# Sparse attention into an ELU MLP on one core: PSUM pairs in neighbouring banks, GpSimd's clamps moved, its fills spread, loads reordered, and a new instruction queue

## The chip, the core and the metric

The kernel runs on one core of a Trainium2 chip. The core has five engines that each take instructions from a queue of their own in order: TensorE (PE, matrix products, with weight loads shown apart as PEld), VectorE (DVE), ScalarE (ACT), GpSimd (POOL) and SyncE (SP). Sixteen DMA engines move data between HBM and the on-chip memory SBUF. Matrix products are written to PSUM, eight banks of 512 float32 columns on 128 partitions. The metric is the time of one execution on the device in microseconds (us), median over runs.

## The reference: what is computed

Attention over 8 batches, 8 heads, 576 positions and 64 channels. Four heads see the last 32 positions, four see the earlier positions at distances that are multiples of 32. Its output is 4608 tokens of 512 channels, and goes through an MLP with an ELU.

```python
scores = (1 / sqrt(64)) * q @ k.T                  # q, k, v: (8, 8, 576, 64) float32
rel = pos[:, None] - pos[None, :]
mask_local   = (rel >= 0) & (rel < 32)             # heads 0 to 3
mask_strided = (rel >= 0) & (pos[None, :] % 32 == pos[:, None] % 32)   # heads 4 to 7
attn = softmax(where(mask, scores, -1e9))
x = (attn @ v) as (4608, 512)
h = x @ w_in                                       # w_in (512, 2048)
g = where(h > 0, h, exp(min(h, 0)) - 1)
out = g @ w_out                                    # w_out (2048, 512), out (4608, 512) float32
```

## The kernel before

Every position is put at a residue, so that the strided heads become dense blocks of 72 by 72 and the local heads become blocks of 96 queries against 128 keys. Attention gives xT, the transposed MLP input, in bf16. The MLP goes over 9 chunks of 512 tokens.

The order of all work is written out by hand in one string, ORDER. Each token of it issues the instructions of one step, and each engine gets its instructions in the order of the tokens. Waits are not written: the framework adds them where one engine's instruction touches what another's has touched. The first letter of a token is the step, and a last number is a PSUM bank or a pair of banks:

- S (scores, L418), e (exp, L425, ACT), m (mask, L432 and L438, DVE), O (values and row sums, L445 to L488), n and r (logarithm and reciprocal of the sums, L516 and L522, ACT), x (product into xT, L547, DVE). Each batch has two strided and two local pairs of heads, each in two halves: S.3l0.1.07 is batch 3, local, pair 0, half 1, in banks 0 and 7.
- a and b, or L (first MLP product, L595; L is both halves, four matmuls), h (exp, L603, ACT), i, j or p (the clamp exp(h)-1 to at most 0, on DVE, ACT or GpSimd: L612 or L610), g (maximum with h, L623, DVE). L.2.5.4 is chunk 2, feature block 5, bank 4.
- Z (second MLP product, L629, four of its sixteen steps: Z.1.3.2.6 is chunk 1, token block 3, part 2, bank 6), o (copy to SBUF, L635, ACT), t (store, L647, SP).
- Ls and Ll load q, k and v of the strided or local heads of a batch, issued on GpSimd. Ts and Tl transpose q and k by DMA, Ks and Kl copy the transposed keys into two zero-padded buffers (kps, kpl). W copies v between its row of ones. T and c, C transpose on TensorE for batches 0 and 1, which have no DMA transposes. w issues products of zeros.

PSUM is one tile of eight banks. A score token, and from batch 2 on a value token, writes two banks, and one exp, logarithm or product reads both as one operand:

```python
    def banks(s):
        i, j = int(s[0]), int(s[1])
        return ps[:, i:j + 1:j - i, 0:W]
```

All raw buffers of a kind are single, so batch b+1 loads after batch b has been transposed. Batch 1 has buffers of its own inside xT and g. Ahead of the queue GpSimd issues the first loads, makes the masks, issues the loads of LOADS (w_in in four parts, w_out in four, batch 1), and then fills the zero and one regions of the padded buffers.

Of the kernel before, what the change touches and what calls it, by code (L numbers as in the profile page):

```python
# [15 lines left out]
S = 576  # L16
D = 64
HG = 4
NS = 8
RS = S // NS  # L20
RP = 80
# [10 lines left out]
LOADS = ['wi0', 'wi1', 'wi2', 'wi3', 'wo0', 'wo1', 'qs1', 'ks1', 'vs1', 'ql1', 'kl1', 'vl1', 'wo2', 'wo3']  # L32
# [8 lines left out]
w.7.28 K.q.1 K.q.0 K.k.1 K.k.0 T.0s0.q.0 c.0s0.q T.0s0.k.1 T.0s1.q.2 c.0s0.k T.0s1.k.3 C.0s1.q  # L41
w.7.1 c.0s1.k S.0s0.0.45 S.0s0.1.67 e.0s0.0 S.0s1.0.01 e.0s0.1 S.0s1.1.23 m.0s0.0 T.0l0.q.4
e.0s1.0 m.0s0.1 O.0s0.0.56 e.0s1.1 c.0l0.q m.0s1.0 n.0s0.0 T.0l0.k.7 m.0s1.1 r.0s0.0 O.0s1.0.01
x.0s0.0 T.0l1.q.4 c.0l0.k n.0s1.0 r.0s1.0 O.0s1.1.23 V.0 S.0l0.0.56 n.0s1.1 x.0s1.0 T.0l1.k.7
c.0l1.q e.0l0.0 O.0s0.1.01 r.0s1.1 c.0l1.k S.0l0.1.45 n.0s0.1 x.0s1.1 w.6.1 r.0s0.1 m.0l0.0
S.0l1.1.67 e.0l0.1 x.0s0.1 S.0l1.0.23 e.0l1.1 m.0l0.1 O.0l0.0.01 e.0l1.0 m.0l1.1 O.0l0.1.45
n.0l0.0 m.0l1.0 O.0l1.1.67 r.0l0.0 n.0l0.1 O.0l1.0.23 x.0l0.0 r.0l0.1 a.0.0.0 n.0l1.0 x.0l0.1
a.0.1.1 r.0l1.0 a.0.2.4 n.0l1.1 x.0l1.0 a.0.3.5 r.0l1.1 a.0.4.2 x.0l1.1 a.0.5.3 b.0.0 b.0.1
h.0.0 b.0.2 h.0.1 b.0.3 i.0.0 g.0.0 b.0.4 h.0.3 b.0.5 i.0.1 h.0.4 a.0.6.6 i.0.3 g.0.1 b.0.6
h.0.5 a.0.7.7 g.0.3 h.0.2 b.0.7 j.0.5 a.0.8.0 i.0.2 i.0.4 a.0.9.1 h.0.6 g.0.4 b.0.8 h.0.7 g.0.5  # L50
a.0.10.5 j.0.7 a.0.11.2 g.0.2 a.0.12.3 h.0.8 g.0.7 b.0.9 j.0.6 b.0.10 i.0.8 h.0.9 g.0.6 b.0.11
h.0.10 b.0.12 g.0.8 a.0.13.4 h.0.12 i.0.10 a.0.14.7 g.0.10 h.0.11 Ll.2 b.0.13 b.0.14 i.0.12
j.0.9 g.0.12 a.0.15.6 h.0.13 T.1s1.k.0 g.0.9 b.0.15 h.0.14 i.0.11 T.1s0.k.5 T.1s0.q.3 g.0.11
h.0.15 Z.0.0.0.1 i.0.13 C.1s0.k i.0.14 T.1s1.q.2 g.0.14 C.1s0.q Z.0.0.1.1 i.0.15 C.1s1.q g.0.13
S.1s0.1.35 T.1l0.q.7 g.0.15 e.1s0.1 c.1s1.k S.1s0.0.24 c.1l0.q T.1l0.k.6 e.1s0.0 m.1s0.1
S.1s1.0.35 V.1 O.1s0.1.07 c.1l0.k e.1s1.0 Ls.2 T.1l1.q.2 n.1s0.1 m.1s1.0 S.1l0.1.46 r.1s0.1
m.1s0.0 C.1l1.q O.1s1.0.35 x.1s0.1 Z.0.0.2.1 n.1s1.0 r.1s1.0 O.1s0.0.07 e.1l0.1 x.1s1.0
T.1l1.k.2 n.1s0.0 m.1l0.1 S.1s1.1.35 r.1s0.0 c.1l1.k Z.0.0.3.1 e.1s1.1 x.1s0.0 Z.0.1.0.4 m.1s1.1
o.0.0 O.1s1.1.26 t.0.0 S.1l1.0.35 n.1s1.1 O.1l0.1.07 r.1s1.1 Z.0.1.1.4 n.1l0.1 x.1s1.1 e.1l1.0
Z.0.1.2.4 r.1l0.1 m.1l1.0 S.1l0.0.12 W.2 Ts.2 S.1l1.1.36 e.1l0.0 x.1l0.1 Z.0.1.3.4 e.1l1.1  # L60
m.1l0.0 O.1l1.0.05 o.0.1 m.1l1.1 O.1l0.0.17 n.1l1.0 O.1l1.1.23 r.1l1.0 Z.0.2.0.6 n.1l0.0 t.0.1
x.1l1.0 r.1l0.0 n.1l1.1 Z.0.2.1.6 x.1l0.0 r.1l1.1 Z.0.2.2.6 x.1l1.1 L.1.0.4 Ks.2 Ls.3 L.1.1.0
h.1.0 L.1.2.5 i.1.0 h.1.1 g.1.0 L.1.3.1 i.1.1 h.1.2 g.1.1 Z.0.2.3.6 p.1.2 h.1.3 i.1.3 S.2s0.0.27
o.0.2 g.1.3 S.2s0.1.34 L.1.4.0 e.2s0.0 t.0.2 g.1.2 e.2s0.1 L.1.5.6 m.2s0.0 h.1.4 m.2s0.1
O.2s0.0.12 j.1.4 L.1.6.7 Tl.2 n.2s0.0 g.1.4 O.2s0.1.35 r.2s0.0 Z.0.3.0.4 n.2s0.1 x.2s0.0
Z.0.3.1.4 r.2s0.1 S.2s1.0.01 h.1.5 L.1.7.2 x.2s0.1 e.2s1.0 i.1.5 L.1.8.3 g.1.5 h.1.7 h.1.6 i.1.7
L.1.9.5 g.1.7 h.1.8 p.1.6 L.1.10.0 m.2s1.0 h.1.9 g.1.6 O.2s1.0.16 h.1.10 Z.0.3.2.4 i.1.8 g.1.8
n.2s1.0 S.2s1.1.27 i.1.10 r.2s1.0 Z.0.3.3.4 Kl.2 Ll.3 g.1.10 e.2s1.1 L.1.11.3 x.2s1.0 o.0.3 Ts.3
m.2s1.1 L.1.12.0 h.1.11 i.1.9 g.1.9 O.2s1.1.27 h.1.12 L.1.13.1 i.1.11 g.1.11 n.2s1.1 S.2l0.0.46
i.1.12 r.2s1.1 L.1.14.5 g.1.12 t.0.3 h.1.13 x.2s1.1 L.1.15.3 e.2l0.0 i.1.13 S.2l1.0.02 m.2l0.0  # L70
h.1.15 S.2l0.1.47 Z.1.0.0.6 g.1.13 e.2l0.1 i.1.15 h.1.14 g.1.15 O.2l0.0.14 Z.1.0.1.6 j.1.14
m.2l0.1 Ks.3 n.2l0.0 g.1.14 O.2l0.1.37 r.2l0.0 Z.1.0.2.6 W.3 n.2l0.1 x.2l0.0 Ls.4 Z.1.0.3.6
r.2l0.1 S.2l1.1.15 e.2l1.0 Z.1.1.0.4 x.2l0.1 e.2l1.1 m.2l1.0 S.3s0.1.02 S.3s0.0.37 o.1.0 m.2l1.1
O.2l1.0.15 e.3s0.0 Z.1.1.1.4 t.1.0 n.2l1.0 m.3s0.0 O.2l1.1.36 Z.1.1.2.4 n.2l1.1 Z.1.1.3.4
r.2l1.1 r.2l1.0 x.2l1.1 Z.1.2.0.7 e.3s0.1 x.2l1.0 O.3s0.0.36 o.1.1 S.3s1.0.02 m.3s0.1 n.3s0.0
L.2.0.1 t.1.1 r.3s0.0 L.2.1.5 h.2.0 x.3s0.0 L.2.2.4 e.3s1.0 i.2.0 g.2.0 h.2.1 L.2.3.3 Tl.3 h.2.2
i.2.1 g.2.1 O.3s0.1.06 h.2.3 S.3s1.1.12 i.2.2 n.3s0.1 L.2.4.5 i.2.3 g.2.2 r.3s0.1 Z.1.2.1.7
g.2.3 h.2.4 x.3s0.1 L.2.5.4 e.3s1.1 Ts.4 i.2.4 L.2.6.3 g.2.4 h.2.5 m.3s1.1 L.2.7.0 i.2.5 h.2.6
g.2.5 O.3s1.1.16 p.2.6 h.2.7 L.2.8.2 m.3s1.0 n.3s1.1 g.2.6 O.3s1.0.45 Z.1.2.2.7 r.3s1.1 W.4
n.3s1.0 x.3s1.1 L.2.9.3 Kl.3 Ll.4 r.3s1.0 Z.1.2.3.7 j.2.7 x.3s1.0 h.2.8 L.2.10.1 g.2.7 Ks.4  # L80
h.2.9 Z.1.3.0.6 o.1.2 i.2.9 g.2.9 h.2.10 t.1.2 S.3l0.0.45 S.3l0.1.07 i.2.10 e.3l0.0 L.2.11.3
g.2.10 e.3l0.1 m.3l0.0 S.3l1.0.45 Z.1.3.1.6 m.3l0.1 e.3l1.0 h.2.11 O.3l0.0.01 m.3l1.0 O.3l0.1.47
L.2.12.5 n.3l0.0 i.2.11 g.2.11 r.3l0.0 Z.1.3.2.6 p.2.8 n.3l0.1 x.3l0.0 L.2.13.3 r.3l0.1 Ls.5
g.2.8 h.2.12 O.3l1.0.01 x.3l0.1 Z.1.3.3.6 n.3l1.0 i.2.12 S.3l1.1.24 r.3l1.0 g.2.12 L.2.14.7
e.3l1.1 x.3l1.0 L.2.15.5 h.2.13 m.3l1.1 o.1.3 Z.2.0.0.2 i.2.13 g.2.13 h.2.14 t.1.3 O.3l1.1.04
h.2.15 Z.2.0.1.2 i.2.14 g.2.14 n.3l1.1 Z.2.0.2.2 i.2.15 r.3l1.1 g.2.15 S.4s0.0.16 x.3l1.1
S.4s0.1.37 e.4s0.0 Z.2.0.3.2 e.4s0.1 m.4s0.0 L.3.0.5 o.2.0 m.4s0.1 L.3.1.0 t.2.0 h.3.0 L.3.2.4
i.3.0 h.3.1 g.3.0 L.3.3.1 i.3.1 h.3.2 g.3.1 Tl.4 O.4s0.0.36 h.3.3 i.3.2 Z.2.1.0.7 g.3.2 n.4s0.0
L.3.4.2 i.3.3 r.4s0.0 g.3.3 Z.2.1.1.7 x.4s0.0 h.3.4 O.4s0.1.05 i.3.4 L.3.5.4 g.3.4 n.4s0.1
Z.2.1.2.7 r.4s0.1 h.3.5 x.4s0.1 S.4s1.0.13 L.3.6.6 e.4s1.0 i.3.5 g.3.5 Z.2.1.3.7 h.3.6 m.4s1.0  # L90
L.3.7.2 i.3.6 o.2.1 g.3.6 O.4s1.0.05 Kl.4 Ll.5 h.3.7 S.4s1.1.13 Z.2.2.0.4 n.4s1.0 i.3.7 g.3.7
t.2.1 L.3.8.7 r.4s1.0 e.4s1.1 x.4s1.0 Ts.5 Z.2.2.1.4 h.3.8 m.4s1.1 L.3.9.6 i.3.8 g.3.8
O.4s1.1.12 h.3.9 S.4l0.0.03 W.5 Z.2.2.2.4 n.4s1.1 L.3.10.5 r.4s1.1 j.3.9 x.4s1.1 Z.2.2.3.4
e.4l0.0 g.3.9 S.4l0.1.17 h.3.10 L.3.11.2 m.4l0.0 o.2.2 i.3.10 O.4l0.0.03 g.3.10 e.4l0.1
Z.2.3.0.6 t.2.2 Ls.6 n.4l0.0 m.4l0.1 Ks.5 L.3.12.4 r.4l0.0 O.4l0.1.15 h.3.11 x.4l0.0 Z.2.3.1.6
n.4l0.1 i.3.11 S.4l1.0.07 g.3.11 r.4l0.1 L.3.13.3 h.3.12 x.4l0.1 Z.2.3.2.6 e.4l1.0 p.3.12 h.3.13
L.3.14.2 m.4l1.0 g.3.12 p.3.13 O.4l1.0.15 h.3.14 S.4l1.1.07 Z.2.3.3.6 g.3.13 n.4l1.0 i.3.14
L.3.15.4 r.4l1.0 g.3.14 e.4l1.1 Z.3.0.0.3 x.4l1.0 o.2.3 m.4l1.1 S.5s0.0.02 h.3.15 Z.3.0.1.3
t.2.3 e.5s0.0 i.3.15 O.4l1.1.17 g.3.15 Z.3.0.2.3 n.4l1.1 m.5s0.0 S.5s0.1.56 r.4l1.1 O.5s0.0.02
Tl.5 Z.3.0.3.3 x.4l1.1 n.5s0.0 Z.3.1.0.4 r.5s0.0 e.5s0.1 x.5s0.0 L.4.0.1 o.3.0 m.5s0.1 L.4.1.7  # L100
h.4.0 t.3.0 L.4.2.5 i.4.0 h.4.1 g.4.0 O.5s0.1.06 i.4.1 h.4.2 L.4.3.2 g.4.1 n.5s0.1 i.4.2
S.5s1.0.13 L.4.4.7 r.5s0.1 g.4.2 h.4.3 x.5s0.1 Z.3.1.1.4 e.5s1.0 i.4.3 L.4.5.5 g.4.3 h.4.4 Kl.5
Ll.6 m.5s1.0 Z.3.1.2.4 h.4.5 i.4.4 g.4.4 O.5s1.0.06 S.5s1.1.13 i.4.5 n.5s1.0 L.4.6.2 Ts.6 g.4.5
r.5s1.0 Z.3.1.3.4 e.5s1.1 x.5s1.0 L.4.7.7 h.4.6 m.5s1.1 o.3.1 i.4.6 O.5s1.1.15 g.4.6 h.4.7
Z.3.2.0.3 t.3.1 n.5s1.1 i.4.7 S.5l0.0.06 g.4.7 r.5s1.1 L.4.8.4 W.6 e.5l0.0 Z.3.2.1.3 x.5s1.1
h.4.8 m.5l0.0 L.4.9.2 i.4.8 g.4.8 Ks.6 Ls.7 O.5l0.0.07 h.4.9 Z.3.2.2.3 n.5l0.0 i.4.9 S.5l0.1.16
g.4.9 L.4.10.5 r.5l0.0 e.5l0.1 x.5l0.0 Z.3.2.3.3 h.4.10 m.5l0.1 L.4.11.4 o.3.2 i.4.10 g.4.10
O.5l0.1.12 t.3.2 h.4.11 S.5l1.0.06 Z.3.3.0.7 n.5l0.1 i.4.11 g.4.11 L.4.12.3 r.5l0.1 e.5l1.0
x.5l0.1 Z.3.3.1.7 h.4.12 m.5l1.0 L.4.13.5 i.4.12 g.4.12 O.5l1.0.04 h.4.13 S.5l1.1.16 Z.3.3.2.7
n.5l1.0 i.4.13 g.4.13 L.4.14.2 r.5l1.0 e.5l1.1 x.5l1.0 Z.3.3.3.7 h.4.14 m.5l1.1 L.4.15.3 o.3.3  # L110
i.4.14 Tl.6 g.4.14 O.5l1.1.15 h.4.15 Z.4.0.0.6 n.5l1.1 i.4.15 S.6s0.0.04 g.4.15 Z.4.0.1.6
r.5l1.1 e.6s0.0 x.5l1.1 S.6s0.1.27 Z.4.0.2.6 e.6s0.1 m.6s0.0 t.3.3 L.5.0.3 m.6s0.1 L.5.1.0 h.5.0
L.5.2.4 i.5.0 h.5.1 g.5.0 O.6s0.0.15 i.5.1 h.5.2 L.5.3.2 g.5.1 n.6s0.0 i.5.2 L.5.4.7 r.6s0.0
# [44 lines left out]
def kernel(  # L158
# [162 lines left out]
    for nm in LOADS:  # L321
        load(nm)
# [374 lines left out]
```

The softmax here doesn't subtract the row's maximum and nothing guards it: scores larger than these inputs give would overflow.

## Time and profile before

| quantity | value |
|---|---|
| time, median of 3 runs | 404.48 us (404.1 to 406.24) |
| span of the profiled run | 403.4 us |
| TensorE busy | 319.4 us, 79% |
| DVE busy | 237.0 us, 59% |
| ACT busy | 228.0 us, 57% |
| GpSimd busy | 106.2 us, 26% |
| mean granted TensorE clock | 0.961 |
| first MLP block, first batch 2 score, last xT product | 20.6, 74.1, ends 330.5 us |

Busy time is the time in which an engine has an instruction in work. In the lines of the profile a name is the program's tile, an arrow points from inputs to output, and "<-" in brackets names what ended the idle time before an instruction. In the view of waits the three numbers are the idle time in total, how often, and the longest.

### The profile page before, as it was taken

How to read it: one execution, taken by the hardware profiler on the slowest of the kernel's cores; microseconds unless marked ns; L12 is line 12 of the kernel's file. 1: busy time of each engine (PE TensorE's matmuls, PEld its weight loads, DVE VectorE, ACT ScalarE, POOL GpSimd, SP SyncE). 2: the span in 40 equal slices, each digit the busy share in tenths (PEclk: the TensorE clock that was granted, in tenths of full speed). 3: DMA queues.
4: the chain of work that ended last, by engine and by line, in shares of the span. 5: the costliest groups of instructions: out<-in, count | busy, mean ns of one | idle time of the engine just before them, and what ended most of it. 6: DMA issues, size and time to landing. Idle time of an engine off the chain costs nothing.

```text
span 403.4 us, 6126 instructions
## 1 busy us (share of the span) xinstructions
PE 319.4 (79%) x2263; PEld 161.2 (40%) x2302; DVE 237.0 (59%) x431; ACT 228.0 (57%) x388; POOL 106.2 (26%) x135
## 2 busy tenths in 40 slices
PE   6896788675778777778577686878988789999995
PEld 5643434332334343344233343434444334444442
DVE  3779835366416866665447665777467649639300
ACT  3785464464546775657556565676667756346121
POOL 8639932155000670432361205200000000000000
PEclk9999598899958999999999999999999999999999
DMA  8999996959714894898199819931421110110132
GB/s 151 189 206 189 132 159 130 156 63 175 117 26 120 125 132 80 137 150 143 49 117 134 165 41 144 83 89 51 99 72 28 26 28 0 48 58 0 53 80 79
DMA packets 110214, 40.59 MB, mean 101 GB/s; under 512 B 91784, under 2 KB 103752, under 8 KB 110184
## 3 DMA queue, kind: packets, MB, share of 16 engines
q0 software_dynamic: 71376, 18.75, 46.6%
q1 hardware_dynamic: 38808, 21.44, 22.8%
q8 instruction: 18, 0.29, 0.3%
q14 instruction: 12, 0.10, 0.1%
HBM read 38.03 MB, written 9.44 MB: 118 GB/s over the span
## 4 chain that ended last, share of the span: by engine, by line
PE 52%; DVE 18%; ACT 15%; DMA 8%; issue 4%; POOL 2%; SPq 0%; ACTq 0%; DVEq 0%; POOLq 0%
PE ps L629 24%; PE ps L595 21%; DVE xT L547 7%; ACT ln L516 6%; DVE g L623 5%; DVE he L612 5%; ACT e L425 4%; PE ps L418 4%; ACT he L603 2%; DMA kl<-in_k_dram 2%; ACT rc L522 2%; DMA kps<-kTs 2%; DMA qTs<-qs 2%; DMA ks<-in_k_dram 1%; PE ps L488 1%
## 5 line engine op out<-in xcount | busy, mean ns | idle before, releaser
L629 PE MATMUL ps<-w_out_sb,g 128*128 128x512 bf16 x557 | 143.6, 390 | 20.5 <-DVE xT L547 8.6
L595 PE MATMUL ps<-xT,w_in_sb 128*128 128x512 bf16 x556 | 137.5, 383 | 16.5 <-DVE xT L547 6.3
L603 ACT ACTIVATE he<-ps 128x512 f32<-128x512 f32 x144 | 84.4, 597 | 46.7 <-PE ps L595 36.0
L623 DVE TENSOR_TENSOR g<-he,ps 128x512 bf16<-128x512 bf16 x136 | 93.2, 687 | 21.7 <-ACT ln L516 7.3
L629 PEld LDWEIGHTS <-g 128*128 128x128 bf16 x576 | 54.4, 100 | 81.9 <-issue 30.7
L595 PEld LDWEIGHTS <-w_in_sb 128*128 128x128 bf16 x576 | 54.8, 98 | 79.7 <-issue 22.8
L612 DVE TENSOR_SCALAR he<-he 128x512 bf16<-128x512 f32 x130 | 64.0, 494 | 29.8 <-ACT he L603 29.4
L547 DVE TENSOR_TENSOR xT<-ps,rc 64x576 bf16<-64x576 f32 (+1 forms) x64 | 43.4, 680 | 62.9 <-ACT e L425 15.8
L425 ACT ACTIVATE e<-ps 72x576 bf16<-72x576 f32 (+1 forms) x64 | 40.9, 647 | 33.5 <-PE ps L418 13.7
L516 ACT ACTIVATE ln<-ps 64x576 f32<-64x576 f32 (+1 forms) x64 | 37.4, 584 | 38.0 <-PE ps L629 10.7
L635 ACT COPY osb<-ps 128x512 f32<-128x512 f32 x36 | 21.1, 585 | 40.1 <-PE ps L629 36.5
L522 ACT ACTIVATE rc<-ln 64x576 f32<-64x576 f32 (+1 forms) x64 | 39.7, 621 | 2.0
L245 POOL DMA_DIRECT2D ql<-in_q_dram x24 | 20.1, 845 | 46.5 <-DMA qTl<-ql 46.5
L612 POOL TENSOR_SCALAR he<-he 128x512 bf16<-128x512 f32 x6 | 12.0, 2004 | 48.8 <-ACT he L603 48.8
L418 PE MATMUL ps<-qTs,kps 128*128 128x72 bf16 x192 | 10.6, 198 | 15.7 <-DVE xT L547 5.7
L252 POOL DMA_DIRECT2D kl<-in_k_dram x24 | 18.1, 786 | 0.0
L432 DVE TENSOR_TENSOR pm<-e,mask_s 72x576 bf16<-72x576 bf16 x32 | 14.5, 461 | 5.9 <-ACT e L425 5.3
L438 DVE TENSOR_TENSOR pm<-e,mask_l 128x576 bf16<-128x576 bf16 x32 | 14.4, 454 | 5.9 <-ACT e L425 5.2
L418 PEld LDWEIGHTS <-kps 128*128 128x128 bf16 x192 | 9.1, 99 | 21.6 <-issue 18.8
L481 PE MATMUL ps<-pm,vsp 72*128 72x72 bf16 x192 | 11.0, 201 | 5.2 <-DVE xT L547 1.6
L481 PEld LDWEIGHTS <-vsp 72*128 72x128 bf16 x192 | 9.9, 101 | 12.6 <-issue 7.4
L418 PE MATMUL ps<-qTl,kpl 128*128 128x96 bf16 x144 | 10.3, 211 | 5.4 <-ACT ln L516 4.1
(87 smaller groups left out, 174.1 us busy)
## 6 DMA issues: line engine op xcount, KB each, us to landing
out_dram<-osb SPq DMA_DIRECT2D x32, 144.0 KB
vl<-in_v_dram POOLq DMA_DIRECT2D x8, 288.0 KB, 6.5
w_in_sb<-in_moe_w_in_dram POOLq DMA_DIRECT2D x4, 512.0 KB, 10.3
w_out_sb<-in_moe_w_out_dram POOLq DMA_DIRECT2D x4, 512.0 KB, 14.8
vs<-in_v_dram POOLq DMA_DIRECT2D x7, 288.0 KB, 7.7
kps<-kTs SPq DMA_DIRECT2D x12, 160.0 KB
ql<-in_q_dram POOLq DMA_DIRECT2D x24, 72.0 KB, 3.5
kl<-in_k_dram POOLq DMA_DIRECT2D x24, 72.0 KB, 3.7
```

What stands on the lines that cost most here:

```text
L418: nc.tensor.matmul(dst, lhsT=kt[pr, k0:k0 + 128], rhs=rhs, start=True, stop=True, skip_group_check=True)
L425: nc.scalar.activation(e[0:R], tiles.pop(("S", key, u))[0:R], ACT.Exp, scale=scale)
L481: nc.tensor.matmul(ov[:, x, j * RS:(j + 1) * RS], lhsT=vs_p[:, c0:c0 + 128], rhs=pm[0:RS, z, n0:n0 + RS], start=True, stop=True, skip_grou ...
L516: nc.scalar.activation(t, s_ps, ACT.Ln)
L522: nc.scalar.activation(t, tiles.pop(("ln", key, u)), ACT.Exp, scale=-1.0)
L547: nc.vector.tensor_mul(dst, o_ps, rc)
L595: nc.tensor.matmul(tiles["h", ch, m], lhsT=w_in_sb[:, c, m * 128:(m + 1) * 128], rhs=xT[:, c, ch * CHUNK:(ch + 1) * CHUNK], start=(c == 2) ...
L603: nc.scalar.activation(e, tiles["h", i[0], i[1]], ACT.Exp)
L612: eng.tensor_scalar(e1, e, scalar1=1.0, scalar2=1.0, op0=ALU.min, op1=ALU.subtract)
L623: nc.vector.tensor_tensor(dst, e1, h, op=ALU.max)
L629: nc.tensor.matmul(ops, lhsT=g[ch % 2][:, m, kk * 128:(kk + 1) * 128], rhs=w_out_sb[:, m, :], start=(m == 0), stop=(m == MC - 1), skip_gro ...
L635: nc.scalar.copy(o_sb, tiles.pop(("o", int(ch), int(kk))))
```

## The change

Five edits that go together:

1. Each pair of banks in ORDER is now two neighbours (i and i+1).
2. The six p tokens, clamps on GpSimd, are i tokens, clamps on DVE.
3. GpSimd's fills are taken apart and issued one after each load from batch 1's first on, rather than all behind the last load. The small loads that fill rows 72 to 79 of q and k (needed by the DMA transposes) move from batch 2's load to behind w_in.
4. All loads of batch 1 are issued ahead of w_out's.
5. The whole queue is ordered anew for this. Products of zeros go from 30 to 62, masks have five buffers for three, clamps three for four.

```diff
-LOADS = ['wi0', 'wi1', 'wi2', 'wi3', 'wo0', 'wo1', 'qs1', 'ks1', 'vs1', 'ql1', 'kl1', 'vl1', 'wo2', 'wo3']
+LOADS = ['wi0', 'wi1', 'wi2', 'wi3', 'qs1', 'ks1', 'vs1', 'ql1', 'kl1', 'vl1', 'wo0', 'wo1', 'wo2', 'wo3']
...
-L.1.3.1 i.1.1 h.1.2 g.1.1 Z.0.2.3.6 p.1.2 h.1.3 i.1.3 S.2s0.0.27
-o.0.2 g.1.3 S.2s0.1.34 L.1.4.0 e.2s0.0 t.0.2 g.1.2 e.2s0.1 L.1.5.6 m.2s0.0 h.1.4 m.2s0.1
+i.1.2 g.1.2 L.1.5.1 h.1.4 i.1.3 g.1.3 j.1.4 Z.0.2.3.7 h.1.5 g.1.4 S.2s0.0.45 o.0.2 S.2s0.1.23
+i.1.5 L.1.6.6 g.1.5 e.2s0.0 t.0.2 e.2s0.1 Z.0.3.0.7 m.2s0.0 h.1.6 m.2s0.1 O.2s0.0.01 L.1.7.2
...
-    p_pm = ctx.enter_context(tc.tile_pool(name="p_pm", bufs=3))
+    p_pm = ctx.enter_context(tc.tile_pool(name="p_pm", bufs=5))
...
-    p_he1 = ctx.enter_context(tc.tile_pool(name="p_he1", bufs=4))
+    p_he1 = ctx.enter_context(tc.tile_pool(name="p_he1", bufs=3))
...
-    for nm in LOADS:
-        load(nm)
-
-    for (c, z), t in kp.items():
...
+    fills = [lambda cz=cz: fill_kp(*cz) for cz in kp]
+    fills += [lambda a=a: fill_ones(*a)
+              for a in ((vl_t[0], HG * LB), (vl_t[1], HG * LB), (vs_p, HG * NS))]
+    for i, nm in enumerate(LOADS):
+        load(nm)
+        if nm == "wi3":
+            for a in (("qs", q), ("ks", k), ("ql", q)):
+                fill_rows(*a)
+        elif i >= 4 and fills:
+            fills.pop(0)()
...
     def load_str(b):
         for nm in ("qs", "ks", "vs"):
             load_runs(nm, int(b))
-        if int(b) == NPE:
-
-            for nm, x in (("qs", q), ("ks", k), ("ql", q)):
-                nc.gpsimd.dma_start(
-                    out=raw[nm][RS:RP].rearrange("p (h f) -> p h f", h=HG),
-                    in_=x[0, 0:HG].rearrange("h (p s) d -> p h (s d)", s=NS)[0:RP - RS])
```

## The prediction

> **What bounds the kernel now.** I read the page's engine shares first, then a table of stages, then what each engine waits for, then the timeline around single gaps.
>
> ```profile
> PE 319.4 (79%) x2263; PEld 161.2 (40%) x2302; DVE 237.0 (59%) x431; ACT 228.0 (57%) x388; POOL 106.2 (26%) x135
> ```
>
> No engine is full. TensorE is nearest, so the question is where it stands still. The stage table (window, its length, busy us and instructions of PE, PEld, DVE, ACT, POOL, granted clock, DMA share, GB/s):
>
> ```profile
> 0.00:20.00 20.00, 14.66 (x248) 12.28 (x250) 11.04 (x30) 11.69 (x22) 15.47 (x29) 1.00 1.16 170
> 20.00:74.00 54.00, 41.43 (x354) 21.18 (x357) 36.27 (x60) 30.44 (x62) 30.57 (x39) 0.87 1.24 167
> 74.00:331.00 257.00, 195.75 (x1357) 97.15 (x1383) 156.78 (x277) 159.74 (x261) 60.11 (x67) 0.97 0.70 96
> 331.00:399.00 68.00, 67.56 (x308) 30.63 (x313) 32.96 (x64) 25.56 (x43) 0.00 (x0) 1.00 0.17 47
> ```
>
> From 331 on only the two MLP products are left and TensorE is full: that stage can't shrink. From 74 to 331, where the attention of batches 2 to 7 runs between MLP blocks, it is idle for over 60 us, with DVE and ACT at 61% and 62% and DMA far below its 1.24. That is the signature of waits, not of work. The view of waits says for whom:
>
> ```profile
> PE ps L629 <- DVE xT L547: 8.6, 7, 2.1
> PE ps L418 <- ACT ln L516: 9.5, 9, 2.0
> PE ps L629 <- ACT e L425: 6.4, 9, 0.9
> PE ps L595 <- DVE xT L547: 6.3, 8, 1.2
> ACT he L603 <- DVE xT L547: 7.4, 7, 2.0
> ```
>
> These are odd pairs. The second MLP product (L629) reads g and w_out; nothing that writes xT or e feeds it. It can wait for them only over a PSUM bank. One such gap on the timeline:
>
> ```profile
> 147.95 0.65 ACT L516 ACTIVATE ln<-ps 64x576 f32<-64x576 f32 x1 [0.57 <-PE ps L629]
> 148.62 0.42 PE L488 MATMUL ps<-pm,vl 128*128 128x96 bf16 x6
> 149.96 0.75 DVE L547 TENSOR_TENSOR xT<-ps,rc 64x576 bf16<-64x576 f32 x1 [1.20 <-ACT he L603]
> 150.76 1.02 PE L629 MATMUL ps<-w_out_sb,g 128*128 128x512 bf16 x4 [1.72 <-DVE xT L547]
> ```
>
> In the queue the xT instruction is x.3l0.1, which reads the pair 47 (banks 4 and 7), and the L629 block is Z.1.3.3.6, which writes bank 6. They share no bank; bank 6 lies between 4 and 7. TensorE stood for 1.72 us until that read ended. I laid the queue's tokens beside the trace's instructions for the whole kernel: in 181 cases the last reader of a pair that merely spans a token's bank ends over 0.1 us after everything that the token truly needs, and in 174 of them the token starts within 0.15 us of that end. So a pair read as ps[:, i:j+1:j-i] counts as all banks from i to j. Of TensorE's 43.3 us between tokens from 125 to 335, 41.7 us end at such a reader; from 60 to 125 it is 10.0 of 14.1. Together 52 us. The slack it destroys is on all engines, so ACT and DVE queues run late too.
>
> Two things cost time before 74. First the fills:
>
> ```profile
> 36.91 5.02 DVE L612 TENSOR_SCALAR he<-he 128x512 bf16<-128x512 f32 x1
> 36.95 1.38 POOL L331 MEMSET vl<- 128x1536 bf16 x1
> 38.35 1.38 POOL L331 MEMSET vl<- 128x1536 bf16 x1
> 39.76 1.80 POOL L331 MEMSET vsp<- 72x2048 bf16 x1
> 42.71 0.64 PE L382 MATMUL ps<-identity,xT 72*128 72x72 bf16 x8 [4.63 <-DVE g L623]
> ```
>
> A clamp that takes 0.42 us elsewhere takes 5.02, exactly while GpSimd fills back to back, and TensorE waits 4.63 us behind it. Second, batch 2's padded keys:
>
> ```profile
> 66.94 7.48 DMA kps<-kTs
> 74.07 0.19 PE L418 MATMUL ps<-qTs,kps 128*128 128x72 bf16 x1 [2.77 <-DMA kps<-kTs]
> ```
>
> **The Trainium skill.** "PSUM — Partial Sum Buffer", section PSUM bank collisions, says to guard by bank; the hardware neither arbitrates nor stalls. The stalls here thus come from waits in the program, and the trace agrees: they end with the reader. "SBUF — State Buffer", Who interferes with whom, says that DVE in a two-port mode (tensor_scalar can enter one) and GpSimd exclude each other for whole instructions; the 5.02 against 0.42 us agrees. "TensorE: Matmul & The Clock Gate", Part 1, says that an idle window of about 3.4 us halves the clock; the 0.87 of stage 20 to 74 agrees.
>
> **The change part by part.**
>
> *Neighbouring pairs.* In the queue before, 83 of the 112 pairs that one instruction reads are wide (j-i over 1); in the new queue none is. The whole class of waits goes: 52 us of TensorE's idle time. But the new queue moves everything else, so I cost the stages from its work, not by subtraction. An MLP block of four matmuls costs 0.86 us where nothing disturbs it (two starts on the timeline):
>
> ```profile
> 345.24 1.03 PE L629 MATMUL ps<-w_out_sb,g 128*128 128x512 bf16 x4
> 346.11 1.03 PE L595 MATMUL ps<-xT,w_in_sb 128*128 128x512 bf16 x4
> ```
>
> A score or value token at full clock takes about 0.28 us (8 matmuls, 86.16 to 86.42 for one).
>
> *To the first score of batch 2.* The new queue has 47.9 us of TensorE work ahead of it; the first MLP block follows 9.8 us of that and can start at about 20.5 as before, since w_in's first quarter lands at 17.6. At full pace TensorE would be there near 59. It is not let: the DMA engines are full to 60 us before, the bytes up to batch 2 are the same, and the key rows for batch 2 must land (58.9 before), be transposed (3.6 us), and be copied to kps (7.5 us beside batch 3's loads). What shortens this chain is that the small row loads, which landed last (61.0) and held the transposes, now come before batch 1: about 2.3 us. So 74.1 becomes 71.8. Loading batch 1 ahead of w_out hides here: its rows land near 35 in place of 40, w_out's first quarter near 38 in place of 27.7, and 17.3 us of work from 20.5 bring TensorE to its first use at 37.8. The fills in pieces save most of the 4.63 us, yet what they free goes into the same wait for kps. I count nothing for them, and 2.5 us against for a halved clock after an idle stretch.
>
> *From there to the end of attention.* 90 + 91 MLP blocks by 0.86 is 155.7, 96 score and value tokens by 0.28 is 26.9: 182.6 us, in 257 us before. What of idle time stays: all TensorE gaps not ended by a spanning reader were under 3 us from 125 to 335, but DVE and ACT queues are now about 142 and 157 us full in a stretch of 200, and first-in first-out queues at 71% and 78% will be late at times. GpSimd's six clamps (2.0 us each, two of them on the chain that ended last) become DVE clamps: 6 by 0.43 = 2.6 us, five of the old ones in this stage, hidden under TensorE. Five pm buffers for three let masks run ahead; three he1 for four costs nothing visible while DVE clamps shortly before it uses them. Padded keys are queued 5 to 15 us of TensorE work ahead of use (2.6 to 17 before), against a copy of 2.4 to 7.5 us. I take 17 us of idle time in all, 8.5%: 199.6 us. Bounds: 3% (188) to 18% (223).
>
> *The rest.* 32 + 41 blocks by 0.86 = 62.8 us, TensorE full. Then the last copy and store: 4.4 us as now.
>
> Sum: 71.8 + 2.5 + 199.6 + 62.8 + 4.4 = 341.1 of span; measured times lie about 1 us above the span (404.48 to 403.4). I say 342.
>
> **Rivals.**
> 1. *Nearly everything comes back.* For it: the queue gives every TensorE token room for its unloaded chain. Idle 3%, and kps at 69: 69 + 188 + 62.8 + 4.4 + 1 = 325. Against: the 78% of ACT.
> 2. *DMA becomes the bound.* DMA is busy some 140 us for batches 3 to 7 between 70 and 265, about 28 to 31 a batch with transposes and copies in series, where TensorE alone would need 29 a batch (144.5 us from batch 2's to batch 7's first score). If copies of 7 us hold the scores, 37 a batch: 71.8 + 5 x 37 = 257; then 101 us of work, 5 idle, 4.4 and 1: 368. Against: the mean share is 0.70 in that stage and kps held TensorE only at the start.
> 3. *True waits replace the false ones by half*, DVE and ACT being late: 26 us of the 52 come back and the startup stays: 342 + 35 = 377.
> 4. *Not faster.* The early stage worsens (w_out late behind GpSimd's pieces, the first half at half clock: +20) and the new order trades the waits one for one: 404 or more. Against: wide pairs are gone, and the work after the last attention is TensorE at full rate in both.
>
> **How the numbers follow.** Forecast 0.52 (332 to 357), rival 1 0.14, rivals 2 and 3 together 0.26 (357 to 385), between these and no change 0.03, rival 4 0.05. The range 325 to 374 takes in the ends of the idle bound (188 and 223 around 199.6) and rival 2, and leaves out rival 1's tail and rival 3. Faster 0.93, same 0.02, slower 0.05.
>
> **What would show it.** Right: waits of L629 and L595 on xT, ln or e shrink to a few us; the stage from batch 2's first score to the last xT is near 200 us, TensorE idle under 10% there; no DVE clamp of 5 us; first batch 2 score near 72, waiting for kps. Wrong: PE's gaps released by kps or qTs in later batches (rival 2), DVE or ACT over 85% busy with PE waiting for pm or g (rival 3), or a start of L629 later than 45 us (rival 4).

## The result and the profile after

The new kernel takes 335.15 us (median of 4 runs, 334.45 to 337.5) against 404.88 us before, a ratio of 0.8285 with a 95% interval of 0.8238 to 0.8332. That is 70 us less, inside the range and 7 us below the forecast of 342.

The page of the new kernel, engine shares, and its stage table with the same columns as before, cut at the same events (first score of batch 2, last xT, last product):

```profile
PE 306.5 (92%) x2295; PEld 159.0 (48%) x2334; DVE 234.2 (70%) x435; ACT 225.5 (68%) x390; POOL 94.2 (28%) x129
```

```profile
0.00:20.00 20.00, 16.73 (x277) 14.02 (x280) 10.28 (x28) 12.53 (x25) 17.94 (x33) 0.72 1.15 167
20.00:72.00 52.00, 40.91 (x368) 20.14 (x370) 37.26 (x66) 31.24 (x64) 26.29 (x35) 0.94 1.36 169
72.00:263.00 191.00, 184.62 (x1370) 96.39 (x1397) 153.34 (x277) 156.18 (x260) 49.95 (x62) 0.99 1.06 133
263.00:329.00 66.00, 64.24 (x288) 28.41 (x291) 33.32 (x65) 25.07 (x43) 0.00 (x0) 1.00 0.15 42
```

The first two stages end at 72, where they ended at 74 before. The third, attention of batches 2 to 7 between MLP blocks, went from 257 to 191 us with the same work: DVE and ACT are busy for about as long as before (153 and 156 us against 157 and 160). What changed is TensorE. Its idle time there fell from 61 us to 6, and its busy time from 196 us to 185. Its granted clock in this stage was 0.97 and is 0.99 now; an estimate from these two means (0.03 of 257 us against 0.01 of 191) puts 6 of the 11 us of busy time down to that. What TensorE waits for over the whole run is this view (engine and line, for whom: us in total, times, longest):

```profile
PE ps L603 <- DVE g L631: 6.6, 8, 4.0
PE ps L432 <- DMA kps<-kTs: 3.1, 3, 2.4
PE ps L603 <- DVE xT L561: 2.4, 2, 2.1
PE ps L396 <- DMA qs<-in_q_dram: 1.4, 1, 1.4
PE ps L637 <- DVE g L631: 1.1, 1, 1.1
```

(The lines moved down by 8 or 14: L595 is L603, L629 is L637, L418 is L432, L547 is L561, L612 is L620, L623 is L631. L382, now L396, is the transposes of batch 1 on TensorE.) The odd pairs are gone. The second MLP product waits for g, which it reads, and no more for xT, ln or e.

### The profile page after: what moved, and what is told of

The parts are those of the page before. It is cut to its first block, busy times and chain, and to the rows that moved or that the text cites. A ratio compares the mean times of both kernels' runs of the same rounds, so it can differ in the third digit from the quotient of the medians.

```text
span 333.3 us, 6205 instructions
## 1 busy us (share of the span) xinstructions
PE 306.5 (92%) x2295; PEld 159.0 (48%) x2334; DVE 234.2 (70%) x435; ACT 225.5 (68%) x390; POOL 94.2 (28%) x129
## 4 chain that ended last, share of the span: by engine, by line
PE 36%; DMA 33%; DVE 11%; POOL 9%; ACT 5%; issue 4%; SPq 1%; DVEq 0%; ACTq 0%; POOLq 0%
PE ps L637 20%; PE ps L603 13%; DMA qTl<-ql 6%; DMA kTs<-ks 6%; DVE g L631 6%; DMA w_in_sb<-in_moe_w_in_dram 4%; DMA vs<-in_v_dram 4%; DMA w_out_sb<-in_moe_w_out_dram 4%; DVE he L620 3%; DMA out_dram<-osb 3%; DMA kTl<-kl 3%; POOL ql L245 2%; DMA kl<-in_k_dram 2%; ACT ln L530 2%; DMA kpl<-kTl 1%
## 5 line engine op out<-in xcount | busy, mean ns | idle before, releaser
L603 PE MATMUL ps<-xT,w_in_sb 128*128 128x512 bf16 x557 | 140.4, 385 | 11.0 <-DVE g L631 6.6
L637 PE MATMUL ps<-w_out_sb,g 128*128 128x512 bf16 x556 | 138.3, 381 | 2.1 <-DVE g L631 1.1
L631 DVE TENSOR_TENSOR g<-he,ps 128x512 bf16<-128x512 bf16 x136 | 93.3, 687 | 6.0
L603 PEld LDWEIGHTS <-w_in_sb 128*128 128x128 bf16 x576 | 54.4, 98 | 72.9 <-issue 16.8
L620 DVE TENSOR_SCALAR he<-he 128x512 bf16<-128x512 f32 x136 | 64.4, 475 | 25.1 <-ACT he L611 24.7
L637 PEld LDWEIGHTS <-g 128*128 128x128 bf16 x576 | 53.1, 98 | 57.4 <-issue 2.4
L561 DVE TENSOR_TENSOR xT<-ps,rc 64x576 bf16<-64x576 f32 (+1 forms) x64 | 43.3, 680 | 25.7 <-ACT rc L536 24.4
L238 POOL DMA_DIRECT2D qs<-in_q_dram x7 | 5.4, 765 | 36.0 <-DMA qTs<-qs 36.0
L432 PE MATMUL ps<-qTs,kps 128*128 128x72 bf16 x192 | 10.3, 197 | 3.5 <-DMA kps<-kTs 3.1
L432 PEld LDWEIGHTS <-kps 128*128 128x128 bf16 x192 | 8.9, 99 | 8.5 <-issue 3.9
L502 PEld LDWEIGHTS <-vl 128*128 128x128 bf16 x144 | 8.7, 97 | 6.2 <-issue 1.0
L432 PEld LDWEIGHTS <-kpl 128*128 128x128 bf16 x144 | 8.5, 97 | 5.8 <-issue 1.2
```

The costliest lines, as they stand in the source:

```text
L432: nc.tensor.matmul(dst, lhsT=kt[pr, k0:k0 + 128], rhs=rhs, start=True, stop=True, skip_group_check=True)
L561: nc.vector.tensor_mul(dst, o_ps, rc)
L603: nc.tensor.matmul(tiles["h", ch, m], lhsT=w_in_sb[:, c, m * 128:(m + 1) * 128], rhs=xT[:, c, ch * CHUNK:(ch + 1) * CHUNK], start=(c == 2) ...
L620: eng.tensor_scalar(e1, e, scalar1=1.0, scalar2=1.0, op0=ALU.min, op1=ALU.subtract)
L631: nc.vector.tensor_tensor(dst, e1, h, op=ALU.max)
L637: nc.tensor.matmul(ops, lhsT=g[ch % 2][:, m, kk * 128:(kk + 1) * 128], rhs=w_out_sb[:, m, :], start=(m == 0), stop=(m == MC - 1), skip_gro ...
```

## The experiments

Times taken on different occasions are compared by their ratio to the kernel before, which ran beside each (405.3, 405.5, 404.9 and 405.1 us). A range in brackets is the 95% interval of the ratio; the new kernel's is 0.8238 to 0.8332.

**Pairs alone: the old queue with neighbours.** Token order, clamps, fills and loads are the old ones. Only bank numbers differ, so chosen that every pair read by one instruction has neighbours.

```diff
-S.1s0.1.35 T.1l0.q.7 g.0.15 e.1s0.1 c.1s1.k S.1s0.0.24 c.1l0.q
+S.1s0.1.23 T.1l0.q.0 g.0.15 e.1s0.1 c.1s1.k S.1s0.0.23 c.1l0.q
```

> The old queue, token for token, with nothing changed but bank numbers: every pair that one instruction reads is made of neighbours. GpSimd's clamps, the fills and the loads are the old ones. Theory A (waits over banks that lie between two far ones are the cost): the stage from batch 2's first score to the last xT falls from 256 to about 195 us, the whole to 338 to 352 us. Rival B (the new order and the other edits bring the gain): 395 to 405 us.

Measured: 343.11 us, ratio 0.8479 (0.8460 to 0.8499). Its row for the stage between batch 2's first score and the last xT, and the top of what TensorE waits for:

```profile
74.00:266.00 192.00, 183.51 (x1384) 94.99 (x1385) 153.28 (x276) 156.85 (x261) 60.83 (x67) 0.99 0.99 130
```

```profile
PE ps L382 <- DVE g L623: 5.1, 2, 4.6
PE ps L418 <- DMA kps<-kTs: 3.6, 3, 2.1
PE ps L418 <- issue: 3.5, 1, 3.5
```

("issue" is time in which nothing that the profile shows held the engine.) The stage took 192 us where the same queue took 257. The 4.6 us behind the fills stay, as they should. So bank numbers alone, with no instruction moved, bring 62 of the 70 us. The banks were chosen anew here, so which token truly waits for which bank changed too; the next run excludes that as the cause.

**Pairs alone, the other way: the new queue with far pairs.** The banks of the new kernel are renamed one for one, which leaves the queue and every true dependence as they are.

```diff
-S.2s0.0.45 o.0.2 S.2s0.1.23 ... Z.0.3.0.7 ... O.2s0.0.01
+S.2s0.0.26 o.0.2 S.2s0.1.15 ... Z.0.3.0.7 ... O.2s0.0.04
```

> The new kernel with its banks renamed one for one (0 1 2 3 4 5 6 7 become 0 4 1 5 2 6 3 7), so that the same queue, with the same true waits, has pairs that are 3 or 4 banks apart. Theory A: 375 to 420 us, with waits of TensorE on xT, ln and e back at 40 us or more. Rival B: 333 to 340 us.

Measured: 406.08 us, ratio 1.0008 (0.9982 to 1.0033), the time of the kernel before. Lines from its view of waits:

```profile
PE ps L432 <- ACT ln L530: 9.9, 14, 1.4
PE ps L603 <- DVE xT L561: 8.8, 10, 1.7
PE ps L432 <- DVE xT L561: 6.4, 6, 1.5
PE ps L432 <- ACT e L439: 6.4, 8, 1.2
PE ps L637 <- ACT ln L530: 4.4, 6, 1.6
```

Waits of score and MLP products on readers of other banks are back. Laid beside the queue, 36.7 of the 40.3 us that TensorE idles between tokens from 74 to 330 end at a reader whose pair merely spans the bank. Everything else the new kernel has (DVE clamps, spread fills, early loads, five pm buffers, the new order) is in this run, and it isn't faster than the kernel before. That doesn't put the rest at nothing: 309 banks lie between its pairs, where 238 lie between those of the kernel before, and the longer false waits can hide a gain of some us.

**A smaller dose.** The banks renamed so that 52 of 112 pairs have one bank between them and the rest stay neighbours (banks 0 to 7 become 0 2 1 3 4 5 7 6).

```diff
-S.2s0.1.23 ... O.1s1.0.01
+S.2s0.1.13 ... O.1s1.0.02
```

> The new kernel with its banks renamed so that 52 of the 112 pairs are two banks apart (one bank between) and 60 stay neighbours; same queue, same true waits. Theory A: between the two ends, in proportion to the banks that lie between (52 here, against 2.0 to 2.7 a pair in the wide renaming): 345 to 365 us. A threshold, or no effect of one bank between: 334 to 338 us.

Measured: 342.17 us, ratio 0.8466 (0.8418 to 0.8514). It is slower than the new kernel, by 7 us, but below what I expected. The far renaming puts 309 banks between pairs (3 for each of 85 pairs, 2 for each of 27) and costs 71 us, 0.23 us a bank; this one has 52 and costs 0.13 us a bank. The cost isn't in proportion. Laid beside the queue, only 2.6 us of TensorE's own idle time end at such readers here. Room in the queue that swallows the first waits would explain that; no run tests it, and where the rest of the 7 us goes is not shown.

**GpSimd's clamps, put back in the new kernel.** Six i tokens become p, issued behind their exp, with the maximum moved later where its bank is free long enough.

```diff
-h.2.5 g.2.4 ... L.2.8.7 j.2.6 i.2.5 g.2.5 h.2.7
+h.2.5 p.2.5 g.2.4 ... L.2.8.7 j.2.6 h.2.7 ... g.2.6 g.2.5
```

> The new kernel with six clamps on GpSimd again (three blocks of chunk 1 and 2 each or the like, 1.2, 1.6, 2.5, 2.8, 3.12, 3.13), each issued right behind its exp and used two maxima later where the banks allow it. Theory A: nothing to see, 334 to 337 us, since TensorE's queue has over 1 us of room there. Rival C (GpSimd's clamps lay on the path and locked DVE out): 2 to 8 us slower, with DVE instructions of over 1 us beside GpSimd's 2 us.

Measured: 341.83 us, ratio 0.8452 (0.8420 to 0.8484), 6.7 us slower. The timeline of GpSimd, DVE and TensorE around one of them (start, length, engine, instructions, what ended the idle time):

```profile
107.26 3.20 POOL L245 DMA_DIRECT2D ql<-in_q_dram  x4 [9.64 <-DMA qTl<-ql]
110.45 3.17 POOL L252 DMA_DIRECT2D kl<-in_k_dram  x4
113.57 1.21 POOL L262 DMA_DIRECT2D vl<-in_v_dram  x1
114.74 0.77 POOL L264 DMA_DIRECT2D vl<-in_v_dram  x1
115.49 3.87 POOL L620 TENSOR_SCALAR he<-he 128x512 bf16<-128x512 f32 x2
...
117.50 0.69 DVE L631 TENSOR_TENSOR g<-he,ps 128x512 bf16<-128x512 bf16 x1 [2.85 <-POOL he L620]
...
118.24 0.41 PE L432 MATMUL ps<-qTl,kpl 128*128 128x96 bf16 x6 [2.90 <-DVE g L631]
```

The clamp's exp ended at 112.6. The clamp started 2.9 us later, since GpSimd was still issuing batch 4's loads, and these had stood 9.6 us behind a transpose. Then DVE waited 2.85 us for the clamp and TensorE 2.90 us for DVE. A clamp takes 2 us, but its queue is one that waits for DMA. The other half of rival C did not come: DVE's instructions beside the six clamps took no longer than elsewhere (0.43 us for a clamp, 0.69 for a maximum).

This is the one clamp of the six that stood so long behind loads, and its wait is not the whole 6.7 us. The stretch behind this wait and the whole stage from the first score of batch 2 to the last xT, in the columns of the stage table:

```profile
119.80:123.10 3.30, 3.30 (x14) 1.34 (x13) 2.81 (x6) 2.87 (x5) 0.00 (x0) 0.51 1.65 163
71.88:269.94 198.06, 188.98 (x1397) 97.43 (x1398) 152.54 (x273) 156.35 (x260) 59.49 (x67) 0.97 0.99 129
```

The stage is 7 us longer than in the new kernel. TensorE is idle for 2.8 us more of it (9.1 against 6.3) and busy for 4.2 us more, at a granted clock of 0.97 where the new kernel has 0.99. The clock was halved right behind the 2.90 us wait, but also for longer at the start of the stage (0.50 from 71.9 to 78.7, where the new kernel has 0.75 over the same length). Whether that part belongs to the clamps is not shown.

**The clamps and the rows in the old queue.** On top of the old queue with near pairs: first the six clamps on DVE at their old places, then also the row loads behind w_in.

```diff
-... Z.0.2.3.3 p.1.2 h.1.3 i.1.3
+... Z.0.2.3.3 i.1.2 h.1.3 i.1.3
```

> The old queue with neighbouring pairs, and the six GpSimd clamps on DVE at the same places in the queue. The clamps' share of the prediction (nothing, hidden under TensorE): 341 to 344 us. Rival C (a GpSimd clamp stands behind load issues that wait for transposes, and the maximum waits for it): 2 to 5 us below the run with near pairs alone, 338 to 341 us.

Measured: 338.12 us, ratio 0.8363 (0.8314 to 0.8411): 1.4% below the run with near pairs alone, and the intervals don't meet. The clamps are worth about 5 us here. In the run with near pairs alone one of them stood behind load issues too: its exp ended at 123.0 and it started at 128.6. How the 5 us come about beyond that is not shown.

```diff
     for nm in LOADS:
         load(nm)
+        if nm == "wi3":
+            for r, x in (("qs", q), ("ks", k), ("ql", q)):
+                nc.gpsimd.dma_start(out=raw[r][RS:RP]..., in_=x[0, 0:HG]...)
```

> The run before, and the small row loads behind w_in as in the new kernel. Theory A: the transposes of batch 2 start some 2.3 us sooner, first score of batch 2 at 72 in place of 74.2, the whole about 2 us below the run before; if TensorE's own arrival held the start, nothing.

Measured: 335.33 us, ratio 0.8296 (0.8255 to 0.8336). First score of batch 2 at 72.8. The interval meets that of the run before, so the 2.8 us of the medians are likely rather than shown. What is shown is the end point: the old queue with near pairs, DVE clamps and early rows takes what the new kernel takes (0.8285). The new order, batch 1 ahead of w_out, the spread fills, the extra zeros and the five pm buffers together bring nothing that can be measured on top.

**The loads of batch 1.** The new kernel with the old order of loads:

```diff
-LOADS = ['wi0', 'wi1', 'wi2', 'wi3', 'qs1', 'ks1', 'vs1', 'ql1', 'kl1', 'vl1', 'wo0', 'wo1', 'wo2', 'wo3']
+LOADS = ['wi0', 'wi1', 'wi2', 'wi3', 'wo0', 'wo1', 'qs1', 'ks1', 'vs1', 'ql1', 'kl1', 'vl1', 'wo2', 'wo3']
```

> The new kernel with the old order of loads (half of w_out ahead of batch 1). Theory A: batch 1 lands some 5 us later, TensorE reaches batch 2's first score later, but that score waits for kps in any case and all bytes ahead of kps are the same: 334 to 338 us, first score of batch 2 at 71 to 74. Rival D (batch 1's landing sets the start): 3 to 6 us slower.

Measured: 336.33 us, ratio 0.8308 (0.8289 to 0.8327), no difference that can be told from the new kernel; first score at 72.9.

**The start, gate by gate.** In the new kernel the fills still hold DVE. Its timeline, DVE, GpSimd and TensorE:

```profile
30.00 4.59 DVE L620 TENSOR_SCALAR he<-he 128x512 bf16<-128x512 f32 x1
...
30.21 1.40 POOL L328 MEMSET vl<- 128x1536 bf16 x1
31.61 0.79 POOL L275 DMA_DIRECT2D w_out_sb<-in_moe_w_out_dram  x1
32.39 1.83 POOL L328 MEMSET vsp<- 72x2048 bf16 x1
...
35.37 2.95 PE L603 MATMUL ps<-xT,w_in_sb 128*128 128x512 bf16 x8 [4.00 <-DVE g L631]
```

The clamp began before the first of these fills and ended with the second, although a load issue lies between the two. TensorE stood for 4.00 us. Five runs ask whether that and the other gates of the start matter. First all fills behind the loads:

```diff
-        elif i >= 4 and fills:
-            fills.pop(0)()
+    for f in fills:
+        f()
```

> The new kernel with GpSimd's seven fills back behind all loads. DVE is held back to back near 36 to 47 us instead of near 30 to 35. Theory A (what is lost before 72 goes into the wait for kps): 334 to 337 us, first score of batch 2 at 72 to 74. Rival E (the spread fills are worth what DVE's hold costs, 4 to 5 us, and batch 2's loads are issued later): 339 to 344 us.

Measured: 336.59 us, ratio 0.8294 (0.8244 to 0.8343), first score at 72.9. Then all fills directly behind w_in, where DVE has no clamps:

```diff
         if nm == "wi3":
+            for f in fills:
+                f()
```

> The new kernel with all seven fills directly behind w_in's loads, from about 13 to 23.5 us, when DVE has no clamps to do; the row loads and batch 1 are issued behind them. The 4.59 us clamp at 30 us goes. Theory A: TensorE reaches batch 2's first score some 4 us sooner and waits for kps 4 us longer: 332 to 336 us. Rival E: 329 to 331 us.

Measured: 336.28 us, ratio 0.8273 (0.8231 to 0.8315), first score at 73.35. The 4.59 us clamp is gone (the longest from 22 to 45 is 0.72), and nothing is gained. Its waits from 20 to 80:

```profile
PE ps L603 <- DVE xT L561: 4.4, 1, 4.4
PE ps L637 <- DVE qTs L407: 3.7, 1, 3.7
PE ps L432 <- DMA kps<-kTs: 1.4, 2, 0.9
```

TensorE comes to its first w_out product sooner (42.0 against 44.4) and stands elsewhere: 3.7 us before that product, 4.4 us before chunk 1. The view names DVE for the first of these, but w_out's first quarter landed at 41.9, so it was the load. My expectation that TensorE would reach the first score 4 us sooner failed: it got there at 72.9 in place of 69.7. Next the strided loads of batch 2, which its first score needs, ahead of the local ones:

```diff
-S.1l0.1.56 Ll.2 n.1s1.0 Ls.2
+S.1l0.1.56 Ls.2 n.1s1.0 Ll.2
```

> The new kernel with batch 2's strided loads (Ls.2) queued ahead of its local ones (Ll.2). The key rows land some 8 us sooner, so kps is there before TensorE. Theory A: the 2.4 us wait for kps goes, TensorE's own arrival near 69.5 sets the start: 331 to 334 us. If kps is not what holds the start: 335 us as before.

Measured: 334.36 us, ratio 0.8207 (0.8159 to 0.8255), first score at 68.8, 3.3 us sooner. By the ratios that is some 3 us less than the new kernel takes, but the intervals meet, so the gain is likely rather than shown. In the profiled run most of it is lost again later, in a wait for batch 4's keys that the new kernel doesn't have:

```profile
130.44 0.40 PE L432 MATMUL ps<-qTs,kps 128*128 128x72 bf16 x7 [3.03 <-DMA kps<-kTs]
```

Then both:

> Both of the two edits before. Theory A (two gates one behind the other, so that only both together pay): first score of batch 2 at 63 to 67, the whole at 326 to 331 us, 2 us or more below the better of the two alone. Rival E (gains add up, none hidden): the sum of the two single gains.

Measured: 332.86 us, ratio 0.8194 (0.8156 to 0.8231), not the 326 to 331 us expected, with the first score at 68.7, not 63 to 67. This interval lies just below the new kernel's. Waits from 20 to 80:

```profile
PE ps L432 <- DMA kps<-kTs: 3.1, 2, 2.4
PE ps L637 <- DMA w_out_sb<-in_moe_w_out_dram: 2.9, 1, 2.9
```

The transposes now run beside the local loads and last 6.8 and 9.6 us, so kps is again what the score waits for. From 80 on TensorE waits another 4.2 us for kps and kpl, where the new kernel waits 0.4. Since w_out now waits too, the last run puts both edits on the old queue with near pairs, DVE clamps and early rows, whose loads bring half of w_out first:

> The old queue with neighbouring pairs, DVE clamps and early rows, and on top of it the seven fills directly behind w_in's loads and batch 2's strided loads ahead of its local ones. Theory A: the 5 us clamp at 37 us and the wait for kps both go, w_out's first half is there before TensorE needs it: first score of batch 2 at 66 to 69, the whole at 328 to 332 us. If the start is held by the loads alone: 335 us as without the two edits.

Measured: 332.96 us, ratio 0.8217 (0.8176 to 0.8259), first score at 68.5 as expected, the time 1 us above the expected range. The wait for w_out is down to 0.7 us, TensorE comes to the first score at 66.3 and waits 2.2 us there. The best of these runs is about 1% below the new kernel. Each removed gate shows the next one; that the bytes which have to land before kps stand behind all of them is likely, but no run shows it.

## Why the prediction was right, and where not

- *The bound and its cause* hold. TensorE stood for readers of pairs that span a bank, and that is shown in both directions: bank numbers alone take the old queue to 343 us and the new one to 406. The first score of batch 2 came at 72.07 (71.8 forecast), and 4.5 us follow the last product (4.4). The products end 65.6 us after the last xT (62.8 forecast): TensorE was not quite full there, busy for 64.2 of 66 us.
- *The stage between* was mis-sized. I took 17 us of idle time on 182.6 us of work, 199.6; it lasted 191.1, so 8.5 us stayed, of which TensorE was idle for 6.3. DVE and ACT are busy for 80% and 82% of the stage (I had 71% and 78%; DVE's 142 us were 153), and yet TensorE seldom waits for them. This term and the 2.5 us for a halved clock, which did not come on top of the first score, take 11 us off the sum. The products give back 2.8, and the time lies 1.7 us above the span in place of 1: that is 335 for 342.
- *GpSimd's clamps* were costed at nothing, hidden under TensorE. That step failed: 5 us in the old queue, 6.7 us put back in the new. I had looked at the clamp's 2 us and not at what its queue does before it, which the traces show for one clamp in each queue; the rest of the cost is open.
- *The fills in pieces* were to save most of the 4.63 us. They did not: 4.00 us stay, moved from 38 to 31, and the sign "no DVE clamp of 5 us" came out at 4.59. That it costs nothing, as forecast, the runs with late and with early fills show.
- *The way to 72* was right in its end and wrong in its middle. I had TensorE near the first score by about 59, waiting a dozen us for kps. It came at 69.7 and waited 2.4 us: its first w_out product was at 44.4 in place of 37.8 (rival 4's sign was 45), and chunk 1 began at 63.5.

```profile
63.50 5.34 PE L603 MATMUL ps<-xT,w_in_sb 128*128 128x512 bf16 x24 [2.07 <-DVE xT L561]
68.68 1.03 PE L637 MATMUL ps<-w_out_sb,g 128*128 128x512 bf16 x4
72.07 0.19 PE L432 MATMUL ps<-qTs,kps 128*128 128x72 bf16 x1 [2.36 <-DMA kps<-kTs]
```

I had counted 47.9 us of TensorE's work ahead of the first score; it was busy for 57.6 us up to 72. Its granted clock was 0.72 up to 20 and 0.94 from there to 72, by an estimate from these 8.7 us of its time (0.28 of 20 and 0.06 of 52). So the halved clock cost more than the 2.5 us set aside for it, and what it cost is hidden in the wait for kps, which set the start as forecast. That TensorE, over 10 us later than I had it, still came before kps, by 2.4 us, is luck.
- *Rival 2* (DMA as the bound) did not come, but it is near. The mean DMA share of the stage is 1.06 where it was 0.70, the page's DMA row stays at nine tenths up to about 208 us, and transposes that took 3.2 to 7.6 us before now take up to 10.8. One of the kernel before, and four of the new one, each from the chain that ended last:

```profile
62.65 3.62 DMA kTs<-ks
```

```profile
66.92 10.55 DMA qTl<-ql
...
85.43 9.39 DMA kTs<-ks
96.17 10.11 DMA qTl<-ql
...
114.61 10.79 DMA kTs<-ks
```

TensorE still waited only 3.1 us for kps in all, but in the runs that gained at the start such waits came back after 80. Of rival 1 the small idle share came nearly (8.5 us are 4.5%, where it said 3% and I 8.5%) and the early kps did not. Rival 3's idle time did not come; of the 35 us it adds, the part beyond the 26 us is not worked out.
- *The clock's condition* as the prediction has it, an idle window of about 3.4 us, does not come out of these traces. With clamps on GpSimd a wait of 2.90 us was followed by half clock (0.51 from 119.8 to 123.1), while with strided loads first a wait of 3.03 us was not (1.00 from 130.5 to 140). What decides is open.

Left open: whether spread fills gain anything where DVE's hold is what sets the time, since here it never did.

## What to carry to other kernels

Look for waits between instructions that share no data, and ask what address range each operand covers for whatever places the waits: an operand with a stride over two far banks blocked all the banks between, and new bank numbers were worth 62 us with no instruction moved. Be wary of a small compute step in a queue whose other work waits for DMA: its cost can be the queue's wait and not its own length. At a start with several gates, removing one shows the next; measure pairs of edits before crediting one.

## What was not expected of the hardware

A DVE clamp that met GpSimd's fills lasted 4.59 us, over two fills and the load issue between them, while in the run with early fills, with load issues alone beside them, clamps stayed between 0.42 and 0.72 us. And the same DMA transposes, 3.2 to 7.6 us long at a mean DMA share of 0.70, lasted up to 10.8 at a share of 1.06; the last two of the new kernel, when few loads were left, took 3.5 and 3.3 us again.
